# Linear attention and two feed-forward layers: small matmuls of attention issued as two halves of the TensorE array

## The chip, the cores and the metric

The kernel runs on one core of a Trainium2 chip. The metric is the device time of one execution in microseconds (us). Before the change it is 977.47 us, the median of 3 runs (977.23 to 977.64).

## The reference

All inputs are float32. q, k and v have shape 4 x 8 x 576 x 64 (batch, heads, positions, head size), omega 128 x 64, and the two layers' weights 512 x 2048 and 2048 x 512.

```
q_s, k_s = q * 64**-0.25, k * 64**-0.25
phi(x) = exp(h - max(h)) / sqrt(128),  h = x @ omega.T - sum(x*x)/2
kv  = phi(k_s).T @ v            # 128 x 64 for each head
z   = sum of phi(k_s) over the positions
att = (phi(q_s) @ kv) / (phi(q_s) @ z + 1e-6)
x   = att with the heads side by side                 # 2304 x 512
y   = relu(x @ w_in)**2 @ w_out
out = elu(y @ w2_in) @ w2_out
```

## The kernel before, in words

Attention is cut into 36 units, 9 for each batch: a k unit and a q unit for each pair of heads, with the first 512 positions, and one l unit with the 64 positions left over of all heads, k and q together. A unit is a [128, 8, 64] tile: 128 positions, and 8 pieces of 64 features, two of which are transposed at a time (`transposed`, L275), so that partitions 0 to 63 of the result hold one piece and partitions 64 to 127 the next. The transposed tile is split in two parts, th and tl, of the faster data type float32r, which together make up a float32.

`projected` multiplies with omega. `omega_limbs` lays omega out twice on the diagonal of a 128 x 256 tile with zeros elsewhere, again in two parts, omh and oml. One matmul with 128 columns of th as weights and the 256 columns of omh as the stream thus projects two pieces. Three products (th omh, tl omh, th oml) add up in one half of a PSUM bank; a unit has 4 such pairs of pieces, 12 matmuls (L292), and two banks, pp 0 and 1, one after the other.

`maxima` reduces each piece on VectorE (L305) and makes the bias nb on GpSimd; `featured` takes the exponential on ScalarE (L321). `used`, for a k unit, multiplies the features with v and a column of ones: 8 float32 matmuls of 65 columns (L340) and one of 130 for the positions left over (L344) add up in one bank, which is copied to kv. For a q unit and an l unit it transposes the features (L358). `attended`, for a q unit, multiplies the transposed features with kv, 8 float32 matmuls of 65 columns (L381), and for every second pair of heads 4 more with 64 weight columns for the positions left over (L398); `normal` divides. `turned` transposes the result for the feed-forward layers (L413, L422).

The order is written out by hand. In every step s each stage works on the unit s - d, in the order of `stages`: transposed (d = 2), weights, featured (4), a feed-forward piece, projected (3), load, maxima (3), squared (1), a feed-forward piece, used (5), turned (7), attended (6), load_v. The feed-forward pieces (`gemm1` at L457, `gemm2` at L508, in the same three products of float32r) run in there from step 33 or 34 on, as soon as a batch is ready; what is left of them follows when the units are done. "weights" is the preparation of the layers' weights on ScalarE and VectorE, a part in each step. All PSUM tiles go through one ring of 8 banks, and most SBUF tiles through one ring of 93 pages.

Of the kernel before, what the change touches and what calls it, by code (L numbers as in the profile page):

```python
# [9 lines left out]
F32R = mybir.dt.float32r  # L10
U32 = mybir.dt.uint32
AF = mybir.ActivationFunctionType
ALU = mybir.AluOpType
AX = mybir.AxisListType
# [3 lines left out]
def linear_attention_two_ffn_kernel(  # L18
# [12 lines left out]
    nc = tc.nc  # L31
    P = 128
    B, H, S, D = q.shape
    M = omega.shape[0]
# [3 lines left out]
    C = S // P  # L38
# [10 lines left out]
    SCALE = float(D) ** -0.25  # L49
    HALF = 0.5 * SCALE * SCALE  # L50
    EPS = 1e-6 * M

    REBIAS = 2.0 ** -112
    assert LH * L == P and C == 4 and H == 4 * LH and 2 * NP * (C * P) == W * H and NP == KD

    const = ctx.enter_context(tc.tile_pool(name="const", bufs=1))
# [7 lines left out]
    def page(shape, name, dt=F32):  # L64
        return pages.tile([P] + list(shape), dt, tag="page", name=name)

    def psum(name):
        return ps.tile([P, W], F32, tag="bank", name=name)

    def flat(t):  # L70
        return t.rearrange("p a b -> p (a b)")

    def minus(eng, out, whole, hi):
        eng.tensor_tensor(out=out, in0=whole, in1=hi.bitcast(F32), op=ALU.subtract)  # L74

    ident = const.tile([P, P], F32, name="ident")
# [96 lines left out]
    om = page([2, D], "om")  # L173
    nc.sync.dma_start(out=om[:, 0, :], in_=omega)
    nc.scalar.dma_start(out=om[:, 1, :], in_=omega)
    omh = const.tile([P, 2 * M], F32R, name="omh")
    oml = const.tile([P, 2 * M], F32R, name="oml")

    p_warm = [None]

    def warm(n):

        if p_warm[0] is None:
            p_warm[0] = psum("p_warm")
        for _ in range(n):
            nc.tensor.matmul(p_warm[0][:, :P], ident, ident, start=True, stop=True)

    def omega_limbs():
        omT = page([2, M], "omT")
        nc.vector.memset(omT, 0.0)  # L190
        warm(4)
        p_om = psum("p_om")
        nc.tensor.transpose(p_om[:, :P], flat(om), ident)
        warm(2)
        for j in range(2):
            nc.vector.tensor_scalar(
                out=omT[j * D:(j + 1) * D, j, :], in0=p_om[j * D:(j + 1) * D, :M], scalar1=SCALE, scalar2=None, op0=ALU.mult
            )
        nc.scalar.copy(out=omh, in_=flat(omT))
        minus(nc.vector, oml, flat(omT), omh)  # L200

    units = []
    for b in range(B):
# [2 lines left out]
    st = {}  # L206
# [75 lines left out]
    def projected(u):  # L282
        b, kind, hp = u
        nm = f"{b}{kind}{hp}"
        th, tl = (st[u].pop(x) for x in ("th", "tl"))
        st[u]["pp"] = []
        for g in range(2):
            pp = psum(f"pp{nm}_{g}")
            for i in range(2):
                cs = slice((2 * g + i) * P, (2 * g + i + 1) * P)  # L290
                for n, (a, o) in enumerate(((th, omh), (tl, omh), (th, oml))):
                    nc.tensor.matmul(  # L292
                        pp[:, i * 2 * M:(i + 1) * 2 * M], a[:, cs], o, start=(n == 0), stop=(n == 2)
                    )
            st[u]["pp"].append(pp)

    def maxima(u):
        b, kind, hp = u
        nm = f"{b}{kind}{hp}"
        sq = sp.tile([P, 8], F32, tag="sq", name=f"sq{nm}")  # L300
        nc.vector.tensor_reduce(out=sq, in_=st[u].pop("s2")[:, :, :D // 2], op=ALU.add, axis=AX.X)
        mx = sp.tile([P, 8], F32, tag="mx", name=f"mx{nm}")
        nb = st[u]["nb"] = sp.tile([P, 8], F32, tag="nb", name=f"nb{nm}")
        for g, pp in enumerate(st[u]["pp"]):
            nc.vector.tensor_reduce(  # L305
                out=mx[:, 4 * g:4 * g + 4], in_=pp.rearrange("p (i m) -> p i m", m=M), op=ALU.max, axis=AX.X
            )

        nc.gpsimd.tensor_scalar(out=sq, in0=sq, scalar1=-HALF, scalar2=None, op0=ALU.mult)
        nc.gpsimd.tensor_tensor(out=mx, in0=mx, in1=sq, op=ALU.add)  # L310
        nc.gpsimd.tensor_tensor(out=nb, in0=sq, in1=mx, op=ALU.subtract)

    def featured(u):

        b, kind, hp = u
        nb = st[u].pop("nb")
        st[u]["ph"] = []
        for g, pp in enumerate(st[u].pop("pp")):
            ph = page([4, M], f"ph{b}{kind}{hp}_{g}")
            for i in range(4):  # L320
                nc.scalar.activation(  # L321
                    out=ph[:, i, :], in_=pp[:, i * M:(i + 1) * M], func=AF.Exp,
                    bias=nb[:, 4 * g + i:4 * g + i + 1],
                )
            st[u]["ph"].append(ph)

    def used(u):

        b, kind, hp = u
        nm = f"{b}{kind}{hp}"  # L330
        phs = st[u]["ph"]
        if kind == "k":
            ll = st[b, "l", 0]
            kv = sp.tile([P, 2, D + 1], F32, tag="kv", name=f"kv{nm}")
            pk = psum(f"pk{nm}")

            for h in range(2):
                o = pk[:, h * (D + 1):(h + 1) * (D + 1)]
                for c in range(C):
                    nc.tensor.matmul(  # L340
                        o, phs[h][:, c, :], st[u]["v"][:, h * C + c, :], start=h == 0 and c == 0, stop=False,
                        skip_group_check=True,
                    )
            nc.tensor.matmul(  # L344
                pk[:, :2 * (D + 1)], ll["ph"][0][:, hp, :], flat(ll["v"][:, 2 * hp:2 * hp + 2, :]),
                start=False, stop=True, skip_group_check=True,
            )
            nc.scalar.copy(out=flat(kv), in_=pk[:, :2 * (D + 1)])
            st[u]["kv"] = kv
            return  # L350
        st[u]["qT"] = []
        for g in range(2):
            if kind == "l" and g == 0:
                continue
            qT = page([4, P], f"qT{nm}_{g}")
            pt = psum(f"pq{nm}_{g}")
            for i in range(4):
                nc.tensor.transpose(pt[:, i * P:(i + 1) * P], phs[g][:, i, :], ident)  # L358
            nc.scalar.copy(out=flat(qT), in_=pt)
            st[u]["qT"].append(qT)  # L360

    def normal(pvs, os, w, nm):
        rd = sp.tile([P, 4 * len(pvs), 1], F32, tag="rd", name=f"rd{nm}")
        rds = [rd[:w, 4 * i:4 * i + 4] for i in range(len(pvs))]
        for pv, r in zip(pvs, rds):
            nc.vector.tensor_scalar(out=r, in0=pv[:, :, D:D + 1], scalar1=EPS, scalar2=None, op0=ALU.add)
        nc.vector.reciprocal(out=rd[:w], in_=rd[:w])
        for pv, o, r in zip(pvs, os, rds):
            nc.vector.tensor_tensor(out=o, in0=pv[:, :, :D], in1=r.to_broadcast([w, 4, D]), op=ALU.mult)

    def attended(u):

        b, kind, hp = u
        if kind != "q":
            return
        xs = page([C, 2, D], f"xs{b}_{hp}")
        pvs = []
        for h in range(2):
            pn = psum(f"pn{b}_{hp}_{h}")
            for c in range(C):  # L380
                nc.tensor.matmul(  # L381
                    pn[:, c * (D + 1):(c + 1) * (D + 1)], st[u]["qT"][h][:, c, :], st[b, "k", hp]["kv"][:, h, :],
                    start=True, stop=True,
                )
            pvs.append(pn[:, :C * (D + 1)].rearrange("p (c d) -> p c d", d=D + 1))
        normal(pvs, [xs[:, :, h, :] for h in range(2)], P, f"{b}_{hp}")
        st[u]["xs"] = xs
        if hp % 2 == 0:
            return
        qd = hp // 2  # L390
        if qd == 0:
            st[b, "xs"] = page([H, D], f"xsl{b}")
        xs = st[b, "xs"]
        qTl = st[b, "l", 0]["qT"][0]
        pn = psum(f"pl{b}_{qd}")
        for i in range(4):
            j, h = 2 * qd + i // 2, i % 2
            nc.tensor.matmul(  # L398
                pn[:L, i * (D + 1):(i + 1) * (D + 1)], qTl[:, j, h * L:(h + 1) * L],
                st[b, "k", j]["kv"][:, h, :], start=True, stop=True,  # L400
            )
        normal([pn[:L, :4 * (D + 1)].rearrange("p (c d) -> p c d", d=D + 1)], [xs[:L, 4 * qd:4 * qd + 4, :]], L, f"l{b}_{qd}")
# [176 lines left out]
    with tc.manual_schedule():  # L579
        load(units[0])  # L580
        load(units[1])
        omega_limbs()
        frames()
        for s in range(1, len(units) + DEPTH):
            if s == 3:
                warm(2)
            for f, d in stages:
# [3 lines left out]
                elif f == "weights":  # L591
                    if s == WEIGHTS - 1:
                        fetch(1)
                    if s >= WEIGHTS:
                        if s >= THREE:
                            cs = ((3, 0), (1,), (4, 2))[s % 3]
                        elif 0 <= s - 6 < len(units) and units[s - 6][1] == "q":
                            cs = (3, 0)
                        else:
                            cs = ((1,), (4, 2))[light[0] % 2]  # L600
# [5 lines left out]
            u = s - DEPTH  # L606
# [36 lines left out]
```

## Time and profile before

| what | value |
|---|---|
| time, median of 3 runs | 977.47 us |
| span of the profiled execution, first to last instruction | 975.3 us |
| TensorE (PE) busy | 968.4 us, 99% of the span |
| weight loads (PEld) busy | 837.1 us, 86% |
| VectorE (DVE) busy | 621.1 us, 64% |
| ScalarE (ACT) busy | 479.2 us, 49% |
| GpSimd (POOL) busy | 91.2 us, 9% |
| chain that ended last, on TensorE | 97% |

The profile is of one execution; its own device time was not recorded, and its span is 2.2 us below the median of the runs. Durations of matmuls overlap, since they are pipelined: the distance from one to the next is shorter than one's duration. It is read from a row that merges a run of them: its length less the duration of one, divided by the count less one. The chain's rows hold the distances themselves.

### The profile page before, as it was taken

How to read it: one execution, taken by the hardware profiler on the slowest of the kernel's cores; microseconds unless marked ns; L12 is line 12 of the kernel's file. 1: busy time of each engine (PE TensorE's matmuls, PEld its weight loads, DVE VectorE, ACT ScalarE, POOL GpSimd, SP SyncE). 2: the span in 40 equal slices, each digit the busy share in tenths (PEclk: the TensorE clock that was granted, in tenths of full speed). 3: DMA queues.
4: the chain of work that ended last, by engine and by line, in shares of the span. 5: the costliest groups of instructions: out<-in, count | busy, mean ns of one | idle time of the engine just before them, and what ended most of it. 6: DMA issues, size and time to landing. Idle time of an engine off the chain costs nothing.

```text
span 975.3 us, 14149 instructions
## 1 busy us (share of the span) xinstructions
PE 968.4 (99%) x5457; PEld 837.1 (86%) x5457; DVE 621.1 (64%) x1130; ACT 479.2 (49%) x1052; POOL 91.2 (9%) x196
## 2 busy tenths in 40 slices
PE   9999999999999999999999999999999999999998
PEld 9999999999888888888888888888888888888886
DVE  6888886574584358435764587558745884485444
ACT  6887885442352234223443366446544654454443
POOL 7455553000000000000000000000000000000000
PEclk9999999999999999999999999999999999999999
DMA  9355420020140013001210022003200220000211
GB/s 249 93 144 140 137 66 2 1 87 1 43 130 1 1 48 104 22 1 44 87 43 1 22 85 68 1 1 101 73 1 0 87 87 1 1 22 13 74 44 65
DMA packets 56610, 53.40 MB, mean 55 GB/s; under 512 B 25568, under 2 KB 50144, under 8 KB 56544
## 3 DMA queue, kind: packets, MB, share of 16 engines
q1 hardware_dynamic: 55696, 52.08, 17.7%
q8 instruction: 43, 0.70, 0.3%
q10 hardware_dynamic: 848, 0.43, 0.2%
q14 instruction: 23, 0.19, 0.1%
HBM read 47.78 MB, written 4.72 MB: 54 GB/s over the span
## 4 chain that ended last, share of the span: by engine, by line
PE 97%; DMA 1%; SPq 1%; ACT 1%; DVE 0%; issue 0%; ACTq 0%
PE ph L457 41%; PE py L508 41%; PE pn L381 3%; PE pk3k L340 1%; PE pk2k L340 1%; PE pk1k L340 1%; PE pk0k L340 1%; PE px L413 1%; PE pp3k L292 1%; PE pp1k L292 1%; PE pp3q L292 1%; PE pp0q L292 1%; PE pp1q L292 1%; DMA ld0k<-in_k_dram 1%; PE pl L398 1%; PE pp0k L292 0%
## 5 line engine op out<-in xcount | busy, mean ns | idle before, releaser
L457 PE MATMUL ph<-xh,wh 128*128 128x512 f32 (+1 forms) x688 | 245.7, 357 | 0.0
L457 PE MATMUL ph<-xl,wh 128*128 128x512 f32 (+1 forms) x688 | 245.7, 357 | 0.0
L457 PE MATMUL ph<-xh,wl 128*128 128x512 f32 (+1 forms) x688 | 245.7, 357 | 0.0
L469 ACT ACTIVATE r<-ph 128x512 f32<-128x512 f32 (+1 forms) x92 | 46.8, 509 | 241.1 <-PE ph L457 241.1
L473 DVE TENSOR_TENSOR gf<-r 128x512 f32<-128x512 f32 (+1 forms) x92 | 53.3, 579 | 154.5 <-ACT r L469 154.1
L457 PEld LDWEIGHTS ph<-xh,wh 128*128 128x128 f32 x688 | 129.3, 188 | 21.3 <-DVE gf L483 0.2
L457 PEld LDWEIGHTS ph<-xl,wh 128*128 128x128 f32 x688 | 129.3, 188 | 21.1
L457 PEld LDWEIGHTS ph<-xh,wl 128*128 128x128 f32 x688 | 129.3, 188 | 20.5
L74 DVE TENSOR_TENSOR gl<-gf,gh 128x512 fp32r<-128x512 f32 (+1 forms) x172 | 105.2, 611 | 47.3 <-ACT gh L484 35.5
L508 PE MATMUL py<-gh,wh 128*128 128x512 f32 (+1 forms) x368 | 127.4, 346 | 0.0
L508 PE MATMUL py<-gh,wl 128*128 128x512 f32 (+1 forms) x368 | 126.8, 345 | 0.0
L508 PE MATMUL py<-gl,wh 128*128 128x512 f32 (+1 forms) x368 | 126.7, 344 | 0.0
L482 DVE SCALAR_TENSOR_TENSOR r<-r,t 128x512 f32<-128x512 f32 (+1 forms) x80 | 51.0, 637 | 105.2 <-ACT t L479 105.2
L508 PE MATMUL py<-wh,gh 128*128 128x512 f32 x288 | 113.7, 395 | 0.0
L508 PE MATMUL py<-wh,gl 128*128 128x512 f32 x288 | 113.5, 394 | 0.0
L508 PE MATMUL py<-wl,gh 128*128 128x512 f32 x288 | 113.3, 393 | 0.0
L477 ACT ACTIVATE gf<-ph 128x512 f32<-128x512 f32 (+1 forms) x80 | 44.4, 555 | 93.5 <-PE ph L457 93.3
L484 ACT CAST gh<-gf 128x512 fp32r<-128x512 f32 (+1 forms) x80 | 46.2, 578 | 82.0 <-DVE gf L483 80.4
L508 PEld LDWEIGHTS py<-gh,wh 128*128 128x128 f32 x368 | 69.2, 188 | 9.4
L508 PEld LDWEIGHTS py<-gh,wl 128*128 128x128 f32 x368 | 69.2, 188 | 9.2
L508 PEld LDWEIGHTS py<-gl,wh 128*128 128x128 f32 x368 | 69.2, 188 | 9.0
L531 DVE TENSOR_TENSOR ya<-py,ya 128x512 f32<-128x512 f32 x108 | 67.2, 682 | 0.6 <-PE py L508 0.6
(325 smaller groups left out, 1460.6 us busy)
## 6 DMA issues: line engine op xcount, KB each, us to landing
st<-in_moe_w_in_dram SPq DMA_DIRECT2D x32, 512.0 KB, 3.6
st<-in_moe_w_out_dram SPq DMA_DIRECT2D x32, 512.0 KB, 3.4
vk<-in_v_dram SPq DMA_DIRECT2D x32, 128.0 KB, 4.2
out_dram<-ya SPq DMA_DIRECT2D x16, 256.0 KB, 2.2
ld0k<-in_k_dram SPq DMA_DIRECT2D x4, 256.0 KB, 4.8
ld0q<-in_q_dram SPq DMA_DIRECT2D x4, 256.0 KB, 4.8
ld1k<-in_k_dram SPq DMA_DIRECT2D x4, 256.0 KB, 4.6
ld1q<-in_q_dram SPq DMA_DIRECT2D x4, 256.0 KB, 4.2
```

Source lines behind the costliest of these rows:

```text
L74: eng.tensor_tensor(out=out, in0=whole, in1=hi.bitcast(F32), op=ALU.subtract)
L292: nc.tensor.matmul(pp[:, i * 2 * M:(i + 1) * 2 * M], a[:, cs], o, start=(n == 0), stop=(n == 2))
L340: nc.tensor.matmul(o, phs[h][:, c, :], st[u]["v"][:, h * C + c, :], start=h == 0 and c == 0, stop=False, skip_group_check=True,)
L381: nc.tensor.matmul(pn[:, c * (D + 1):(c + 1) * (D + 1)], st[u]["qT"][h][:, c, :], st[b, "k", hp]["kv"][:, h, :], start=True, stop=True,)
L457: nc.tensor.matmul(ph[:, :n], wt[:, cs], x_part(xt, moe, i, c)[:, n0:n1], start=(m == 0), stop=(m == 3 * KD - 1))
L469: nc.scalar.activation(out=r, in_=ph[:, :n], func=AF.Relu)
L473: nc.vector.tensor_tensor(out=gf, in0=r, in1=r, op=ALU.mult)
L477: nc.scalar.activation(out=gf, in_=ph[:, :n], func=AF.Relu, scale=-1.0)
L482: nc.vector.scalar_tensor_tensor(out=r, in0=r, scalar=1.0, in1=t, op0=ALU.add, op1=ALU.mult)
L484: nc.scalar.copy(out=gh, in_=gf)
L508: nc.tensor.matmul(y, *((w[:, ts], a) if moe == 0 else (a[:, ts], w)), start=j == 0 and m == 0 and t % per == 0, stop=j == GF - 1 and m == ...
L531: nc.vector.tensor_tensor(out=ya_t[i, t], in0=yv, in1=ya_t[i, t], op=ALU.add)
```

## The change

The projections use omega once, scaled, on 128 partitions: omega's transpose stands in partitions 0 to 63 and again in 64 to 127, with no zeros. Each of the 12 matmuls of 128 rows and 256 columns becomes two of 64 rows and 128 columns, one in the upper and one in the lower half of the array's rows, issued in turns; the upper half writes bank pp 0, the lower bank pp 1. The pieces therefore lie in the banks in another order, which `maxima` (a stride of 2), `featured` (another column of nb) and `phi` follow.

The float32 products with kv and v (L340, L344, L381) are issued as two halves of 64 weight columns each, in turns, which write partitions 0 to 63 and 64 to 127 of the same bank. L398, the transposes and the feed-forward layers stay as they are.

```diff
--- before.py
+++ after.py
@@ -49,6 +49,8 @@
     SCALE = float(D) ** -0.25
     HALF = 0.5 * SCALE * SCALE
     EPS = 1e-6 * M
+    ROWS = (slice(0, D), slice(D, 2 * D))
+    HALVES = (slice(0, P // 2), slice(P // 2, P))
 
     REBIAS = 2.0 ** -112
     assert LH * L == P and C == 4 and H == 4 * LH and 2 * NP * (C * P) == W * H and NP == KD
@@ -173,8 +175,8 @@
     om = page([2, D], "om")
     nc.sync.dma_start(out=om[:, 0, :], in_=omega)
     nc.scalar.dma_start(out=om[:, 1, :], in_=omega)
-    omh = const.tile([P, 2 * M], F32R, name="omh")
-    oml = const.tile([P, 2 * M], F32R, name="oml")
+    omh = const.tile([P, M], F32R, name="omh")
+    oml = const.tile([P, M], F32R, name="oml")
 
     p_warm = [None]
 
@@ -186,18 +188,14 @@
             nc.tensor.matmul(p_warm[0][:, :P], ident, ident, start=True, stop=True)
 
     def omega_limbs():
-        omT = page([2, M], "omT")
-        nc.vector.memset(omT, 0.0)
+        omT = page([M], "omT")
         warm(4)
         p_om = psum("p_om")
         nc.tensor.transpose(p_om[:, :P], flat(om), ident)
         warm(2)
-        for j in range(2):
-            nc.vector.tensor_scalar(
-                out=omT[j * D:(j + 1) * D, j, :], in0=p_om[j * D:(j + 1) * D, :M], scalar1=SCALE, scalar2=None, op0=ALU.mult
-            )
-        nc.scalar.copy(out=omh, in_=flat(omT))
-        minus(nc.vector, oml, flat(omT), omh)
+        nc.vector.tensor_scalar(out=omT, in0=p_om[:, :M], scalar1=SCALE, scalar2=None, op0=ALU.mult)
+        nc.scalar.copy(out=omh, in_=omT)
+        minus(nc.vector, oml, omT, omh)
 
     units = []
     for b in range(B):
@@ -283,16 +281,12 @@
         b, kind, hp = u
         nm = f"{b}{kind}{hp}"
         th, tl = (st[u].pop(x) for x in ("th", "tl"))
-        st[u]["pp"] = []
-        for g in range(2):
-            pp = psum(f"pp{nm}_{g}")
-            for i in range(2):
-                cs = slice((2 * g + i) * P, (2 * g + i + 1) * P)
-                for n, (a, o) in enumerate(((th, omh), (tl, omh), (th, oml))):
-                    nc.tensor.matmul(
-                        pp[:, i * 2 * M:(i + 1) * 2 * M], a[:, cs], o, start=(n == 0), stop=(n == 2)
-                    )
-            st[u]["pp"].append(pp)
+        pps = st[u]["pp"] = [psum(f"pp{nm}_{g}") for g in range(2)]
+        for i in range(4):
+            cs = slice(i * P, (i + 1) * P)
+            for n, (a, o) in enumerate(((th, omh), (tl, omh), (th, oml))):
+                for pp, r in zip(pps, ROWS):
+                    nc.tensor.matmul(pp[:, i * M:(i + 1) * M], a[r, cs], o[r, :], start=(n == 0), stop=(n == 2))
 
     def maxima(u):
         b, kind, hp = u
@@ -303,7 +297,7 @@
         nb = st[u]["nb"] = sp.tile([P, 8], F32, tag="nb", name=f"nb{nm}")
         for g, pp in enumerate(st[u]["pp"]):
             nc.vector.tensor_reduce(
-                out=mx[:, 4 * g:4 * g + 4], in_=pp.rearrange("p (i m) -> p i m", m=M), op=ALU.max, axis=AX.X
+                out=mx[:, g::2], in_=pp.rearrange("p (i m) -> p i m", m=M), op=ALU.max, axis=AX.X
             )
 
         nc.gpsimd.tensor_scalar(out=sq, in0=sq, scalar1=-HALF, scalar2=None, op0=ALU.mult)
@@ -320,31 +314,34 @@
             for i in range(4):
                 nc.scalar.activation(
                     out=ph[:, i, :], in_=pp[:, i * M:(i + 1) * M], func=AF.Exp,
-                    bias=nb[:, 4 * g + i:4 * g + i + 1],
+                    bias=nb[:, 2 * i + g:2 * i + g + 1],
                 )
             st[u]["ph"].append(ph)
 
+    def phi(u, n):
+        return st[u]["ph"][n % 2][:, n // 2, :]
+
     def used(u):
 
         b, kind, hp = u
         nm = f"{b}{kind}{hp}"
-        phs = st[u]["ph"]
         if kind == "k":
             ll = st[b, "l", 0]
             kv = sp.tile([P, 2, D + 1], F32, tag="kv", name=f"kv{nm}")
             pk = psum(f"pk{nm}")
 
             for h in range(2):
-                o = pk[:, h * (D + 1):(h + 1) * (D + 1)]
                 for c in range(C):
-                    nc.tensor.matmul(
-                        o, phs[h][:, c, :], st[u]["v"][:, h * C + c, :], start=h == 0 and c == 0, stop=False,
-                        skip_group_check=True,
-                    )
-            nc.tensor.matmul(
-                pk[:, :2 * (D + 1)], ll["ph"][0][:, hp, :], flat(ll["v"][:, 2 * hp:2 * hp + 2, :]),
-                start=False, stop=True, skip_group_check=True,
-            )
+                    for m in HALVES:
+                        nc.tensor.matmul(
+                            pk[m, h * (D + 1):(h + 1) * (D + 1)], phi(u, h * C + c)[:, m], st[u]["v"][:, h * C + c, :],
+                            start=h == 0 and c == 0, stop=False, skip_group_check=True,
+                        )
+            for m in HALVES:
+                nc.tensor.matmul(
+                    pk[m, :2 * (D + 1)], phi((b, "l", 0), hp)[:, m], flat(ll["v"][:, 2 * hp:2 * hp + 2, :]),
+                    start=False, stop=True, skip_group_check=True,
+                )
             nc.scalar.copy(out=flat(kv), in_=pk[:, :2 * (D + 1)])
             st[u]["kv"] = kv
             return
@@ -355,7 +352,7 @@
             qT = page([4, P], f"qT{nm}_{g}")
             pt = psum(f"pq{nm}_{g}")
             for i in range(4):
-                nc.tensor.transpose(pt[:, i * P:(i + 1) * P], phs[g][:, i, :], ident)
+                nc.tensor.transpose(pt[:, i * P:(i + 1) * P], phi(u, 4 * g + i), ident)
             nc.scalar.copy(out=flat(qT), in_=pt)
             st[u]["qT"].append(qT)
 
@@ -378,10 +375,11 @@
         for h in range(2):
             pn = psum(f"pn{b}_{hp}_{h}")
             for c in range(C):
-                nc.tensor.matmul(
-                    pn[:, c * (D + 1):(c + 1) * (D + 1)], st[u]["qT"][h][:, c, :], st[b, "k", hp]["kv"][:, h, :],
-                    start=True, stop=True,
-                )
+                for m in HALVES:
+                    nc.tensor.matmul(
+                        pn[m, c * (D + 1):(c + 1) * (D + 1)], st[u]["qT"][h][:, c, m], st[b, "k", hp]["kv"][:, h, :],
+                        start=True, stop=True,
+                    )
             pvs.append(pn[:, :C * (D + 1)].rearrange("p (c d) -> p c d", d=D + 1))
         normal(pvs, [xs[:, :, h, :] for h in range(2)], P, f"{b}_{hp}")
         st[u]["xs"] = xs
```

## Rows read from the trace of the kernel before

**Rows 1.** The page: span, busy time by engine, granted clock in 40 slices.

```profile
span 975.3 us, 14149 instructions
...
PE 968.4 (99%) x5457; PEld 837.1 (86%) x5457; DVE 621.1 (64%) x1130; ACT 479.2 (49%) x1052; POOL 91.2 (9%) x196
...
PEclk9999999999999999999999999999999999999999
```

**Rows 2.** The page: shares by engine of the chain that ended last.

```profile
PE 97%; DMA 1%; SPq 1%; ACT 1%; DVE 0%; issue 0%; ACTq 0%
```

**Rows 3.** Windows: stretch, length, busy us (instructions) by engine, clock, DMA.

```profile
11.00:135.00 124.00, 123.43 (x1093) 121.30 (x1094) 105.05 (x236) 104.95 (x331) 70.98 (x146) 1.00 0.50 136
135.00:190.00 55.00, 55.00 (x482) 54.49 (x482) 34.62 (x82) 32.74 (x101) 13.72 (x28) 1.00 0.07 20
190.00:975.00 785.00, 780.44 (x3834) 652.49 (x3832) 475.95 (x805) 338.03 (x617) 0.00 (x0) 1.00 0.13 42
```

**Rows 4.** Waits from 20 to 130 us: total us, times, longest.

```profile
ACT th2q L278 <- PE pt2q L275: 3.4, 2, 2.7
...
PEld pq2q L358 <- DVE xl L74: 0.5, 1, 0.5
PEld pp2k L292 <- ACT ph2k L321: 0.5, 2, 0.3
```

**Rows 5.** Instructions of L292, L381, L398: ns min/median/max, starts, weights' shape, stream's shape.

```profile
L292 PEld LDWEIGHTS pp1k<-omh,th1k x16: 187/189/192, 38.8 to 69.7; 128*128 128x128 f32 x16
L292 PE MATMUL pp1k<-omh,tl1k x16: 274/282/286, 39.0 to 69.9; 128*128 128x256 f32 x16
...
L381 PEld LDWEIGHTS pn<-kv1k,qT1q x64: 191/192/192, 63.3 to 92.0; 128*128 128x128 f32 x64
L381 PE MATMUL pn<-kv1k,qT1q x64: 221/275/275, 63.4 to 92.1; 128*128 128x65 f32 x64
...
L398 PEld LDWEIGHTS pl<-kv1k,qT1l x16: 133/138/139, 74.0 to 92.7; 128*64 128x64 f32 x16
L398 PE MATMUL pl<-kv1k,qT1l x16: 219/222/271, 74.0 to 92.7; 128*64 128x65 f32 x16
```

**Rows 6.** The chain in order of time: start, length in us, what, count.

```profile
5.71 5.39 DMA ld0k<-in_k_dram
...
42.47 1.73 PE pn L381 x16
44.20 0.44 PE pt1q L275 x4
44.64 1.42 PE pp1l L292 x12
...
49.22 1.73 PE pk1k L340 x16
51.23 1.73 PE pn L381 x16
52.97 0.61 PE pl L398 x8
53.57 0.59 PE pt1q L275 x4
```

**Rows 7.** Timeline of TensorE from 72 us: start, length of the merged run.

```profile
72.19 1.90 PE L381 MATMUL pn<-kv1k,qT1q 128*128 128x65 f32 x16
74.02 0.68 PE L398 MATMUL pl<-kv1k,qT1l 128*64 128x65 f32 x8
74.63 0.66 PE L275 MATMUL pt2k<-ident,ld2k 128*128 128x128 f32 x4
```

**Rows 8.** Timeline of TensorE from 95 us, around a change to 64 rows.

```profile
95.27 0.60 PE L413 MATMUL px<-ident,xs 128*128 128x128 f32 x4
95.80 0.46 PE L422 MATMUL pxl<-ident,xsl 64*128 64x64 f32 x4
96.19 0.66 PE L275 MATMUL pt2k<-ident,ld2k 128*128 128x128 f32 x4
```

## The prediction

> **What bounds the kernel now.** Read the page first: TensorE is busy for 99% of a span of 975.3 us, at the full granted clock in every slice [rows 1], and the chain that ended last is 97% TensorE [rows 2]. So the bound is what TensorE issues. The span and what lies around it make the time: the median of the runs shown is 977.47 us, so I carry 2.2 us around the span and give the result as 977.5 plus a sum.
>
> The change touches attention alone, so the windows come next [rows 3]. From 11 to 135 us TensorE does attention with almost no feed-forward work beside it: 123.4 of 124 us busy, but DVE and ACT are each at 105 (85%). From 135 to 190 us attention is interleaved with feed-forward steps and DVE and ACT are near 60%. From 190 us on nothing is changed. The waits say the same: in the first stage ACT has stood waiting for TensorE up to 2.7 us at a time, and TensorE for ACT or DVE about 0.5 us in all at each place [rows 4].
>
> The decisive view is one line's instructions, with the chain in order of time. A float32 matmul is two records (L381: 16 records for 8 matmuls) [rows 5, 6]. L381 and L398 stream the same 128x65 operand. With 128 weight columns sixteen records take 1.73 us, 108 ns each; with 64 weight columns eight take 0.61 us, 76 ns, of which some is a start that is paid once (below). The timeline gives the bare step: (0.68 - 0.222)/7 = 65 ns with that start in it [rows 7], so about 58 without. The weight load takes 192 ns for 128 columns and 138 for 64, 54 ns less [rows 5]. So L340 and L381 are paced by loading weights, about 54 ns per 64 columns, and the 65 streamed columns hide under it. The projections (L292) go at 1.42/12 = 118 ns [rows 6], their load (188 ns, 128 columns) just under a stream of 256 columns: two nearly equal bounds.
>
> **The change part by part.**
>
> *Column halves, L340 and L381.* 32 units (16 k, 16 q) of 8 matmuls: 256, at 1.73/8 = 216 ns. Each becomes two with 64 weight columns, each two records of 58 ns. If the halves load and stream side by side, a pair costs 2 x 58 = 116 ns: 256 x (116 - 216) = -25.6 us. If their loads go one after the other, 4 x 59 = 236 ns: 256 x 20 = +5.1 us. Nothing in the trace alternates two halves, so both ends stay open. I take the lower, because the records are paced per weight column, and two halves have different columns.
>
> *The leftover product, L344.* 16 matmuls at 0.28 us (the gap between L340's end at 50.95 and L381's start at 51.23) [rows 6]. 130 streamed columns are twice 65, so about 232 ns if side by side, 464 if not: -0.8 or +2.9 us. I take the first, with the same answer as above.
>
> *Row halves, L292.* 36 units x 12 = 432 matmuls of 256 columns become 432 pairs of 128. Each half still loads 128 weight columns, so even side by side a pair can't go under a 128-column load, some 112 ns by L381's steps: 432 x (112 - 118) = -2.6 us. Halving the streamed columns buys nothing there; the load takes over at once. One after the other it is 224 ns: 432 x 106 = +45.8 us. I take side by side, since the halves read different partitions, but this is the term where being wrong costs most.
>
> *Changing the shape of the array.* The trace holds such changes: L398 (128x64) and L422 (64x128). From L381's last start, 72.19 + 1.90 - 0.275 = 73.82, to L398's first at 74.02 are 205 ns where the step is 112: +93; the first load stands uncovered as well, some 50 more. On the way out, four transposes take 0.59 us instead of 0.44 [rows 6]: +0.15. L413 to L422 gives 95.27 + 0.60 - 0.273 = 95.60 to 95.80, the same 0.2 us for row shapes, and 0.66 against 0.60 behind it [rows 8]. I take 0.145 us a change. Counting in the code: 36 projections in and out are 72; used(k) and attended(q) follow each other, so 17 column groups are 34; in the 13 steps below 33 where a projection runs straight into used(k), one change serves for two, so 93. L398's 16 changes vanish, being inside a group now: 77 net, +11.2 us. If the wait ends sooner behind these shorter matmuls it is 77 x 0.093 = 7.2; with a 128-column load uncovered each time, 77 x 0.2 = 15.4.
>
> *Small edits.* The dropped memset and the single scaling of omega lie beside the first loads (the chain starts with the k load, which lands at 11.1 us [rows 6]): 0, at most a few tenths either way. Cost on DVE of reading the maxima out with a stride and of ACT's other bias column: 0, as the sizes are the same. Both PSUM banks of a projection are now taken at its start and complete at its end, so one is asked for, and the other handed on, six matmuls (0.7 us) earlier and later. ACT's 2.7 us of waiting is the cover; without it, 0.7 us where ACT is late. TensorE already waits there for ACT's exponentials (0.5 us, twice) [rows 4]; I put 0 to 4 us in the range. No DMA and no queue's order is moved; loads issue as TensorE frees pages.
>
> *Sum on TensorE:* -25.6 - 0.8 - 2.6 + 11.2 = -17.8 us.
>
> *What is late next.* Some 11.5 of the 16 k-q pairs fall before 135 us, so -12.8 us of it there: 124 becomes 111 us, with DVE and ACT still needing 105, that is 94%. They were the waiting ones and will be waited for, through the eight PSUM banks. I let two thirds through, -8.5 us (ends: 3 and 12.8), and all 5.0 after 135 us, where they are at 60%. Total -13.5 us: 964 us.
>
> The trace shows a changed shape to cost a wait with nothing loaded ahead, and shows loads and streams overlapping only within one shape. The Trainium skill (TensorEngine Tiling (Array Packing), Key Properties) says that different tiles load weights and multiply in parallel, by which the sum stays at -17.8. But it also says (TensorE: Matmul & The Clock Gate, Part 3, The mechanism) that a weight load overlaps running matmuls only if its row group differs, and column halves share their rows. L398, 128 rows throughout, steps at 58 ns while its load and stream need 54 each, so by the letter the rule fails here; between two column halves no run so far shows it. By it the column terms would be the rival's below.
>
> **Rivals.**
> 1. *Row halves side by side, column halves not.* Both column halves read the same partitions for weights and for the stream, so a port may take them in turn; each load in the trace is alone on its engine. Against: the load time scales with columns, not rows. It decides as soon as a column pair costs over about 170 ns, as then the saving (256 x 46 = 11.8) no longer pays the changes of shape. Price: +5.1 + 2.9 - 2.6 + 11.2 = +16.6, all of it on TensorE: 994 us.
> 2. *Row halves' loads one after the other, columns side by side.* L292's load is already the near-equal bound, and 24 of 112 ns would need 2.69 us a unit for 1.42: -25.6 - 0.8 + 45.8 + 11.2 = +30.6: 1008 us. A stream of 128 columns in this data type going slower per column than one of 256 (no row has under 256) gives about the same.
> 3. *No tile overlaps another:* +45.8 + 5.1 + 2.9 + 11.2 = +65: 1042 us.
> 4. *The gain is real but doesn't get out:* column pairs in between, or ACT and DVE holding the first stage at 124 us, leaving -5 of the later stage and eaten by the banks: about 976 to 979 us.
>
> **How the numbers follow.** Forecast 0.51 (own range 955 to 971), rival 1 0.20, rival 2 0.10, rival 3 0.10, rival 4 0.09. Within 0.2% (975.5 to 979.4, about what a measurement here can tell from no change) holds most of rival 4: 0.08. Faster: the forecast and a little of rival 4, 0.52; slower: rivals 1 to 3, 0.40. The range from 953 to 1000 holds the forecast, rivals 4 and 1 and leaves out the two dearest.
>
> **What would show it.** A pair of column halves at 116 ns (used(k) of 16 matmuls near 0.95 us where eight took 1.73) confirms the main term, 236 rival 1. A projection of 24 near 1.35 us plus a change of shape confirms the row term, 2.7 rival 2. Gaps of about 0.1 us at each change of shape, and TensorE waits for ACT's exponentials or casts between 11 and 135 us with ACT and DVE above 90%, confirm what is late next. The span from 190 us on should be as long as before; if it isn't, the prediction misses something. It is wrong altogether if loads of different tiles never lie side by side.

## The result and the profile after

| | before | changed |
|---|---|---|
| time, median (range) | 977.36 us (977.23 to 977.64) | 968.55 us (965.85 to 971.8) |
| span of the profiled execution | 975.3 us | 967.9 us (its time: 969.72 us) |

The ratio is 0.9909, with a 95% interval of 0.9887 to 0.9932: 8.8 us faster. The forecast was 964.0 us, the range 953 to 1000. One number stands out beside the median: the changed kernel's four runs lie 6 us apart, those of before 0.4.

The page of the changed kernel (span, busy by engine, granted clock by slice, chain by engine), which answers to [rows 1, 2]:

```profile
span 967.9 us, 16095 instructions
...
PE 954.9 (99%) x6433; PEld 814.3 (84%) x6433; DVE 623.4 (64%) x1128; ACT 479.1 (50%) x1052; POOL 90.6 (9%) x196
...
PEclk8999999999999999999999999999999999999999
...
PE 91%; DVE 5%; ACT 1%; DMA 1%; issue 1%; SPq 0%; POOL 0%; POOLq 0%; ACTq 0%; DVEq 0%
```

DVE is on the chain now, with 5%, where it had 0%. The windows, as [rows 3]:

```profile
11.00:135.00 124.00, 118.80 (x1907) 109.07 (x1908) 109.15 (x243) 107.91 (x340) 72.58 (x151) 0.96 0.55 146
135.00:190.00 55.00, 54.31 (x686) 52.16 (x685) 37.22 (x88) 32.10 (x97) 10.78 (x23) 1.00 0.01 2
190.00:967.00 777.00, 773.09 (x3768) 645.07 (x3767) 471.17 (x790) 334.96 (x610) 0.00 (x0) 1.00 0.14 43
```

In the first stage TensorE is idle for 5 of 124 us, DVE and ACT do more in the same time, and the granted clock is 0.96 on the mean. The chain in order of time, where [rows 6] stood:

```profile
36.56 0.46 PE pl L396 x8
37.02 0.59 PE pt1k L273 x4
37.61 1.48 PE pp0q L289 x24
39.09 1.02 PE pq0q L355 x8
...
42.48 1.09 PE pk0k L336 x32
43.78 0.93 PE pn L379 x32
44.72 0.59 PE pt1q L273 x4
```

L379 is the old L381: 8 pairs of halves in 0.93 us, 116 ns for the four records of a pair, where 8 matmuls on the whole array took 1.73. L336 (the old L340) needs 1.09 with the change of shape in front of it, and the gap from its end at 43.57 to 43.78 is L341 (the old L344) at 0.21 for 0.28. L289, the projections, need 1.48 for 1.42, the change of shape included. The transposes behind a changed shape pay the way out: 1.02 behind L289 and 0.59 behind L379, where they took 0.87 and 0.44. The row of the kernel before for the 0.87:

```profile
46.06 0.87 PE pq0q L358 x8
```

The timeline of the changed kernel shows the two row halves of a projection start together, a pair every 0.11 us:

```profile
37.70 0.28 PE L289 MATMUL pp0q<-omh,tl0q 64*128 64x128 f32 x2
37.81 0.28 PE L289 MATMUL pp0q<-oml,th0q 64*128 64x128 f32 x2
37.93 0.27 PE L289 MATMUL pp0q<-omh,th0q 64*128 64x128 f32 x2
```

From 53 us on the chain of the changed kernel holds stretches in which DVE follows DVE:

```profile
75.93 0.60 DVE wl L76
76.53 0.60 DVE cv L141
77.13 0.33 DVE sq1q L295
77.46 1.20 DVE mx1q L299 x2
78.65 0.60 DVE xl L76
79.25 0.60 DVE tl2l L76
```

wl and cv are the preparation of the feed-forward weights, the others attention's own. And TensorE's waits over the whole span (total, times, longest), against the short ones of [rows 4]:

```profile
PE pt0k L273 <- DMA ld0k<-in_k_dram: 2.4, 1, 2.4
...
PE pp2q L289 <- ACT ph2q L315: 1.3, 2, 0.7
PE pp1q L289 <- ACT ph1q L315: 0.7, 1, 0.7
...
PE ph L455 <- DVE xl L76: 0.7, 1, 0.7
```

From attention's last transposes on, which start at 192.85 us before and at 185.07 in the changed kernel, both need the same time to the end, 782.5 and 782.8 us. So the whole difference lies in attention, which is what the prediction asked of the span from 190 us on.

### The profile page after: what moved, and what is told of

Its sections match the earlier page's. It is cut to its first block, busy times and chain, and to the rows that moved or that the text cites. A ratio compares the mean times of both kernels' runs of the same rounds, so it can differ in the third digit from the quotient of the medians.

```text
span 967.9 us, 16095 instructions
## 1 busy us (share of the span) xinstructions
PE 954.9 (99%) x6433; PEld 814.3 (84%) x6433; DVE 623.4 (64%) x1128; ACT 479.1 (50%) x1052; POOL 90.6 (9%) x196
## 4 chain that ended last, share of the span: by engine, by line
PE 91%; DVE 5%; ACT 1%; DMA 1%; issue 1%; SPq 0%; POOL 0%; POOLq 0%; ACTq 0%; DVEq 0%
PE py L506 42%; PE ph L455 41%; PE pn L379 1%; PE pp0q L289 1%; DMA ld0k<-in_k_dram 1%; PE pk0k L336 1%; PE pp3k L289 0%; PE pp0k L289 0%; PE px L411 0%; PE pq0q L355 0%; DVE cv L141 0%; DVE xl L76 0%; DMA st<-in_moe_w_in_dram 0%; PE pq3q L355 0%; PE pp2q L289 0%
## 5 line engine op out<-in xcount | busy, mean ns | idle before, releaser
L455 PEld LDWEIGHTS ph<-xh,wh 128*128 128x128 f32 x688 | 129.3, 188 | 23.1 <-DVE xl L76 0.8
```

The source lines that it names most:

```text
L455: nc.tensor.matmul(ph[:, :n], wt[:, cs], x_part(xt, moe, i, c)[:, n0:n1], start=(m == 0), stop=(m == 3 * KD - 1))
```

## The experiments

**Each part alone.** Column halves alone keep the projections of before:

```diff
-                    nc.tensor.matmul(
-                        o, phs[h][:, c, :], st[u]["v"][:, h * C + c, :], ...
+                    for m in HALVES:
+                        nc.tensor.matmul(
+                            pk[m, h * (D + 1):(h + 1) * (D + 1)], phs[h][:, c, m], ...
...   (L344 and L381 in the same way)
```

> The float32 products in column halves, the projections as before. Theory (a pair of column halves costs 116 ns instead of 216, row halves gain nothing and cost two changes of shape a unit): TensorE's work falls by 24 us, 6 more than with both parts; attention up to 135 us is then held by DVE and ACT as it is with both parts, so most of the extra shows only after 135 us: 960 to 966 us, at least 3 us below the changed kernel. Rival (both parts bring a share of the gain, the row halves by streaming half the columns): above 968.5 us.

Measured: 963.21 us (963.03 to 963.37), ratio 0.9858 [0.9846, 0.9871]. That is 5.3 us below the changed kernel with both parts, so the row halves cost time; a part of the 5.3 goes through the clock, as the next experiment shows. Row halves alone are the changed kernel with one "half":

```diff
-    HALVES = (slice(0, P // 2), slice(P // 2, P))
+    HALVES = (slice(0, P),)
```

> The projections in row halves, the float32 products on the whole array as before. Theory: a pair of row halves is paced by one load of 128 columns, 111 ns for 118, and each of the 36 units pays two changes of shape of 0.145 us: 36 x (0.29 - 0.08) = +7.5 us on an engine that sets the time there: 983 to 986 us, slower than before. Rival (half the streamed columns, half the time): 36 x 0.7 us less, about 955 to 965 us.

Measured: 989.29 us (985.11 to 994.85), ratio 1.0128 [1.0095, 1.0161]. Slower, as the theory had it, and the rival is out; but the median is 12 us over before, where 7.5 were expected, and the six runs scatter over 10 us. They fall into two groups: three at 985.1 to 985.3 us, 8.2 us over before, with a mean granted clock of 0.999 or 1.0, and three at 993.3 to 994.9 with 0.99. The profile is of one with 0.99. The chain of row halves alone:

```profile
64.58 1.49 PE pp1k L289 x24
66.07 0.59 PE pq1l L355 x4
...
71.02 1.49 PE pp1k L289 x24
72.50 1.93 PE pk1k L336 x16
```

24 halves need 1.49 us for 1.42, and what follows them 0.15 (0.59 for 0.44) or 0.20 (1.93 for 1.73) more: 0.22 to 0.27 a unit, 8 to 10 us in 36. The rest of the time of these three is in the windows of the same kernel (10 to 20 us, 20 to 30 us; the column behind POOL is the granted clock):

```profile
10.00:20.00 10.00, 9.08 (x70) 8.35 (x68) 4.45 (x9) 6.11 (x22) 6.70 (x14) 0.64 1.13 302
20.00:30.00 10.00, 10.00 (x70) 9.11 (x72) 4.46 (x9) 6.92 (x21) 4.61 (x10) 0.51 0.66 156
```

The clock was at its lower level, 1.2 GHz, from 12.8 to 29.8 us of that execution.

**The clock at the start.** The four runs of the changed kernel follow their mean granted clock: 965.85 us at 0.999, 967.37 at 0.998, 969.72 at 0.995 and 971.8 at 0.99. The profile is of the third, and the clock was at its lower level from 12.1 to 18.9 us:

```profile
10.00:20.00 10.00, 7.56 (x84) 6.50 (x84) 3.95 (x8) 5.55 (x19) 6.28 (x13) 0.66 1.01 263
20.00:30.00 10.00, 10.00 (x169) 9.21 (x169) 7.63 (x17) 10.00 (x34) 6.10 (x15) 1.00 0.80 209
```

Before it, TensorE had stood still from 10.3 to 12.7 us, waiting for the load of the second k unit (the expectations call it the third k load). The next kernel puts work there:

```diff
             if s == 3:
                 warm(2)
+            if s == 5:
+                p_warm[0] = None
+                warm(10)
```

> Both parts, with ten more matmuls of the identity (2.2 us) issued where TensorE waited 2.4 us for the third k load, at 10.3 us; they compute nothing that is used. Theory (that wait let the granted clock fall to 0.5 from 12.1 to 18.9 us, which cost about 3.4 us and makes the changed kernel's runs scatter by 6 us): the clock stays at 1.0 up to 20 us, and the runs lie closer together at 965 to 967 us. Rival (the time was lost to the late load alone, or the scatter comes from the later stretch that DVE and ACT hold): 968 to 970 us as before the extra matmuls.

Measured: 967.17 us (966.69 to 967.41), ratio 0.9897 [0.9883, 0.9912]: the scatter of 6 us is 0.7 us, and the clock between 10 and 20 us is 1.00:

```profile
10.00:20.00 10.00, 10.00 (x144) 9.11 (x142) 6.74 (x13) 7.96 (x29) 7.08 (x15) 1.00 1.10 299
```

So the fall at the start makes the scatter and some 1.4 us of the median. The expectation had put 3.4 us on it, and the time lies 0.2 us above the range of its theory. That the wait alone caused it does not stand: column halves alone stood still there for 1.46 us, row halves alone for only 0.92, and of these two the clock fell for the row halves.

The changed kernel lost the clock a second time, from 104.2 to 107.7 us. The window around it and two rows of the chain:

```profile
100.00:108.00 8.00, 6.67 (x74) 6.00 (x68) 6.11 (x15) 7.15 (x23) 7.01 (x14) 0.79 0.77 193
```

```profile
104.86 1.90 PE pq2q L355 x8
...
106.76 0.85 PE px L411 x4
```

At the full clock these took 1.02 and 0.44 us; with the projection in front (1.79 for some 1.49) and the transposes behind (0.52 for 0.44) the fall cost some 1.7 us. Before it, TensorE had waited 0.63 us for ACT's exponentials, issued one matmul of a row half and waited another 0.71 us. The kernel with ten more matmuls loses the clock there too, from 102.7 to 106.2 us. Column halves alone do not, though TensorE stood still for 0.91 us at the same projection.

The same ten matmuls were put into row halves alone.

> Row halves alone, with ten more matmuls of the identity (2.2 us), which compute nothing that is used, where TensorE waits for the third k load at 10.4 us. Row halves alone took 985.1 to 994.9 us, and in their profile the granted clock was 0.5 from 12.8 to 29.8 us. Theory (the clock fell because TensorE, with half the array's rows at a time, then stood still for 0.9 us; with whole-array work in that place it stays up): 984 to 987 us in every run, so 7.5 to 9 us over before, which is the two changes of shape in each of 36 units. Rival (row halves let the clock fall by themselves, wait or no wait): the runs scatter over 5 us or more and the median stays near 989 us.

Measured: 986.70 us (986.51 to 986.75), ratio 1.0097 [1.008, 1.0114]. No scatter: 9.5 us over before, against the 8 to 10 us of the rows above. With whole-array work in that gap the clock stayed at 1.00; whether any other work there would have done the same was not separated.

**Halves without turns.** The loops over the halves go outside, so all of one half comes first:

```diff
+        for pp, r in zip(pps, ROWS):
-        for i in range(4):
-            cs = slice(i * P, (i + 1) * P)
-            for n, (a, o) in enumerate(((th, omh), (tl, omh), (th, oml))):
-                for pp, r in zip(pps, ROWS):
+            for i in range(4):
+                cs = slice(i * P, (i + 1) * P)
+                for n, (a, o) in enumerate(((th, omh), (tl, omh), (th, oml))):
...   (and `for m in HALVES` outside in used and attended)
```

> Both parts, but all matmuls of one half first and then all of the other. Theory (the halves overlap because the next weight load goes to the other half while this half's load and stream still run, which needs them in turns): every load waits for the one before in its half, 224 ns for two row halves and 116 + 116 ns for two column halves: projections 2.7 us and used(k) about 1.9 us, in all some +60 us: about 1035 to 1045 us. Rival (TensorE's sequencer looks far enough ahead, or the halves overlap in any order): as the changed kernel, 966 to 972 us.

Measured: 1012.59 us (two runs), ratio 1.0364 [1.0346, 1.0382]. Slower by 44 us than in turns, but not by the 70 expected: neither side was right. Some of the 44 is the clock again: the profile has it at the lower level from 9.4 to 23.1 us, which at half the speed costs up to 7 us, an estimate. The timeline of one projection, from its ninth matmul on:

```profile
64.62 0.27 PE L289 MATMUL pp1q<-oml,th1q 64*128 64x128 f32 x1
64.63 0.38 PE L289 MATMUL pp1q<-omh,th1q 64*128 64x128 f32 x2
64.79 0.32 PE L289 MATMUL pp1q<-omh,tl1q 64*128 64x128 f32 x2
64.90 0.33 PE L289 MATMUL pp1q<-oml,th1q 64*128 64x128 f32 x2
65.01 0.27 PE L289 MATMUL pp1q<-omh,th1q 64*128 64x128 f32 x1
65.13 0.27 PE L289 MATMUL pp1q<-omh,tl1q 64*128 64x128 f32 x1
```

Nine matmuls go singly, 111 ns apart, then three pairs side by side, then nine singly. So the second half begins while the first still has three to go: in this trace TensorE starts matmuls three places before their turn. The chain of this kernel has 24 halves in 2.44 us, where 1.48 is all side by side and 2.69 all singly:

```profile
63.74 2.44 PE pp1q L289 x24
66.18 1.66 PE pk1k L336 x29
```

**What holds the first stage.** Three kernels, one run each, without weight preparation beside attention, told by 20 units: from the start of the fourth k unit's transposes (the expectations call it the fifth) to the first k unit's of the last batch.

```diff
-    WEIGHTS, THREE, FIRST, TWO = 4, 18, 33, 34
+    WEIGHTS, THREE, FIRST, TWO = 999, 18, 33, 34
```

> Column halves alone, and the preparation of the feed-forward weights taken out of attention's steps (it is done when the first feed-forward step asks for it, so the end is late and the whole time says nothing). Read: from the fifth k unit's start to the first k unit of the last batch, 20 units, which took 89.7 us before the change, 83.6 in the changed kernel and 81.3 with column halves alone. Theory (what is missing there is held by DVE and ACT, which prepare weights beside attention): TensorE sets the pace again, nine k-q pairs by 1.43 us less than before: 77 us, with TensorE busy throughout. Rival (the pace is set by the chain through the eight PSUM banks or by the steps' order, not by how much DVE and ACT have to do): 80 to 82 us.

> The changed kernel with the same move of the weights' preparation; the whole time again says nothing. The same 20 units, 83.6 us in the changed kernel. Theory (DVE and ACT hold it): TensorE's own work, nine pairs by 1.0 us less than before and two l units by 0.2 more: 81 us. Rival (PSUM banks, order): 83 to 84 us.

> The kernel before, with the preparation of the feed-forward weights taken out of attention's steps as in the two kernels that were read this way (the whole time says nothing). The same 20 units took 89.7 us before, and 77.9 us in the changed kernel without the preparation. Theory (the step sums from the chain are right, and the kernel before was itself held a little by DVE, ACT and a load): 77.9 + 8.6 = 86 to 87 us. Rival (nothing but TensorE set the pace before; the sums are 3 us short): 89 to 90 us.

| 20 units | with preparation | without | held |
|---|---|---|---|
| before | 115.45 - 25.75 = 89.70 us | 115.23 - 26.87 = 88.36 us | 1.3 us |
| both parts | 112.25 - 28.61 = 83.64 us | 102.18 - 24.29 = 77.89 us | 5.8 us |
| column halves | 105.62 - 24.32 = 81.30 us | 98.40 - 23.73 = 74.67 us | 6.6 us |

The windows from 25 to 100 us without preparation, column halves alone first, then both parts, then the kernel before:

```profile
25.00:100.00 75.00, 75.00 (x1101) 72.70 (x1100) 63.51 (x157) 69.09 (x225) 48.78 (x103) 1.00 0.48 132
```

```profile
25.00:100.00 75.00, 75.00 (x1273) 69.30 (x1275) 61.30 (x148) 67.01 (x219) 47.12 (x99) 1.00 0.43 115
```

```profile
25.00:100.00 75.00, 75.00 (x672) 73.98 (x671) 55.12 (x133) 58.26 (x191) 40.63 (x86) 1.00 0.36 94
```

TensorE never stands still in any of them. All the steps and banks are as they were, so the preparation held the rest, and not the order or the banks alone. These kernels take the loads of the weights out of the stretch as well. That it is the load of DVE and ACT rests on this: no wait of TensorE between 20 and 130 us names a DMA, in the changed kernel or in column halves alone, and the next experiment, which leaves those loads in place, gains by relieving DVE.

The 83.64 us of both parts hold the second fall of the clock. Without its 1.7 us some 4.1 would be held; the other five stretches have the clock at 1.00 throughout. The values came lower than expected (77, 81) and, for before, between the two sides. A count of what falls between the two starts explains it: 9 used(k), 9 attended, 5 with L398, 20 projections. By the chain's rows that is 9 x (1.30 - 2.01) + 9 x (0.93 - 1.73) = -13.6 for the columns, 20 x 0.07 + 11 x 0.15 = +3.1 for the projections and 4 x 0.15 - 5 x 0.15 = -0.2 for the other changes of shape: -10.7 us, where 88.36 - 77.89 = 10.5 was measured, and -13.8 for columns alone, where 13.7 was measured. The 1.0 us a pair of the expectation was a sum done too roughly.

**Relieving the two engines.** On column halves alone:

```diff
-        minus(nc.vector, l, tf, h)
+        minus(nc.vector if alone[0] else nc.gpsimd, l, tf, h)
```

> Column halves alone, and the last of the five operations that prepare a weight tile, the low part, on GpSimd instead of DVE while attention runs (16 tiles of 0.6 to 1.0 us each on DVE, about 1 us on GpSimd, which is 60% busy there). Theory (DVE is the engine that holds the first stage, ACT as much): DVE is relieved of some 8 us before 135 us, ACT of nothing: 1 to 4 us less than column halves alone, 959.5 to 962.5 us. Rival (GpSimd's short operations for the exponentials' bias queue behind the 1 us ones, and ACT waits): 963 to 967 us.

Measured: 959.04 us (958.91 to 959.42), ratio 0.9814 [0.9799, 0.9829], the best of all, 4.2 us below column halves alone and 9.5 below the changed kernel. The theory held, half a us beyond its range, though the expectation had miscounted: there are 8 such tiles in attention, not 16, at 1.3 us each on GpSimd:

```profile
L75 POOL TENSOR_TENSOR wl<-cv,wh x8: 1274/1302/1844, 50.5 to 130.0; 128x512 fp32r<-128x512 f32 x8
```

With the rescaling on GpSimd too:

```diff
+        if alone[0]:
             nc.scalar.activation(out=staged[p][1], in_=src, func=AF.Copy, scale=REBIAS)
+        else:
+            nc.gpsimd.tensor_scalar(out=staged[p][1], in0=src, scalar1=REBIAS, ...
```

> As the kernel before it, and also the first operation, the rescaling (0.7 us each on ACT), on GpSimd while attention runs. Theory: both engines that hold the first stage are relieved, DVE by some 8 us and ACT by some 8 us, GpSimd goes to about 75%: 956 to 960 us, with 20 units in 78 to 80 us. Rival (the bias operations on GpSimd come late): 963 us or more.

Measured: 965.31 us (964.76 to 965.41), ratio 0.9878 [0.9861, 0.9894]. Here the rival won. Waits from 20 to 120 us:

```profile
ACT ph2k L326 <- POOL nb2k L316: 4.4, 4, 1.6
ACT ph1k L326 <- POOL nb1k L316: 3.3, 4, 1.4
ACT ph0k L326 <- POOL nb0k L316: 2.2, 2, 1.4
```

ACT, which was to be relieved, waits for the bias that GpSimd makes behind the rescalings, of which each takes 1.54 us there: 13.2 us in all such rows of this stretch, against 3.1 in the kernel before it.

## Why the prediction was right, and where it was off

*Column halves side by side:* right. 116 ns a pair was forecast and 0.93/8 = 116 measured. Rival 1 is out. One line of the Trainium skill (TensorE: Matmul & The Clock Gate, Part 3, The mechanism) lets a weight load overlap running matmuls only where the row group differs; two column halves share their rows, and 8 pairs in 0.93 us overlap all the same. The trace disagrees with that line, as L398 had let expect. The same section also has loads pulled ahead into a background weight buffer; no run here shows whether that is what happens.

*Row halves paced by one load of 128 columns:* right, 0.11 us a pair, and with two changes of shape a loss: 8.2 to 9.5 us alone where the clock stayed up, 5.3 in company, the falls of the clock included. The prediction had -2.6 for the pairs and left the 72 changes of shape in the common +11.2, so it did not say that this part alone loses. The experiment does.

*Changes of shape:* right at about 0.145 us, by the rows for L289 and what follows it.

*The sum on TensorE*, -17.8 us: right. By the chain's rows -24.2 for the columns, +2.5 and 23 x 0.15 = +3.5 for the projections and nothing for the rest give -18.2.

*What is late next:* the engines were named rightly, and so nearly was the size. The step let two thirds through in the first stage (-8.5); over the 20 units it was 6.1 of 10.5, 58%. Without the second fall of the clock it would be 7.8 of 10.5, 74%. The prediction has no term for the clock, here or at the start. Its 0 to 4 us for the two banks that a projection now takes together show up as well: at 64.4 and at 102.1 us one row half begins, and the rest waits 0.71 us each time for ACT's exponentials.

*The start:* this step failed. The small edits were put beside the first loads at 0, or a few tenths. In the profiled execution the second k unit's load landed at 12.6 instead of 11.1 us, and with the clock at its lower level until 18.9 us the third q unit began 4.2 us late (24.36 for 20.16). Over the runs this lower clock is worth 968.55 - 967.17 = 1.4 us. Why the load landed later is open; it was issued at the same time, and in the four kernels with column halves alone TensorE took it up at 10.1 to 11.7 us.

*Two readings* in the prediction are off, without weight in the sum. The step that it takes as 112 ns is (1.90 - 0.275)/15 = 108 by its row, and a pair of row halves measured 111. And the wait that it gives as 0.5 us, twice, is 0.5 us in all over two, and of the weight load.

Together for the profiled execution: -18.2 on TensorE, +4.2 at the start, and 4.4 us more than before in the 20 units (2.7 held by DVE and ACT, 1.7 the second fall of the clock) leave, by subtraction, some 2.2 us around them to make the -7.4 of its span. What makes these 2.2 us was not taken apart.

## What to carry to other kernels

Before splitting a matmul over halves of the array, look at whether its step follows the weight columns or the streamed columns. Halving the weight columns halved the step here; halving the rows bought 7 ns of 118 and cost two changes of shape. Group what runs in one shape, and issue the halves in turns. And when the busiest engine is relieved, read how much room the next two have in that very stage: a quarter of what this change won there came back as waits, and more through the lower clock behind them. Moving one operation to an engine with room returned 4 us; moving a second one gave them away and 2 us more, since something short and urgent was queued behind it.

## What the runs showed of the hardware that was not expected

Matmuls of two halves need not start in the order of the program: without turns, three of the second half ran beside the last three of the first (9 single, 3 pairs, 9 single). And the granted clock fell at a wait of 0.92 us behind row halves, and after two of 0.63 and 0.71 us, not at one of 1.46 us in the kernel whose projections use the whole array; without turns it fell at 9.4 us, with no wait over 0.31 us since 5 us. This window of that kernel, 10 to 20 us, has TensorE busy throughout at half the clock:

```profile
10.00:20.00 10.00, 10.00 (x53) 9.22 (x52) 4.39 (x8) 5.33 (x18) 4.73 (x10) 0.50 1.15 308
```

Matmuls on half of the rows are what these executions have in common before the clock fell; whether it is that or something else of the row halves was not separated. Row halves in turns were not enough for it: with the gap at the start filled, the kernel with row halves alone kept the clock at 1.00 through all 36 projections.
